# The gate column multiplied with the keys instead of the values, and the gate row loaded and transposed later

## Chip, cores, metric

One core of one Trainium2 chip. The metric is the device time of one execution in microseconds (us).

## The reference, cut to what matters

```python
# x: [1, 2048, 640]; 32 heads of 20
g = sigmoid((x * gate_w).sum(-1, keepdims=True))      # one number per token
a = A(x, wqkv, w_phi, wo)     # linear attention: q, k, v projections, softmax features of q and k
b = B(x, w_gate, w_up, w_down)                        # SwiGLU feed-forward, 640 -> 1728 -> 640
return g * a + (1 - g) * b
```

The gate needs one dot product of length 640 per token. The kernel gets it nearly free: gate_w is appended as a 641st column to a weight matrix that multiplies x anyway. The question is which matrix carries the column, and when the column is made.

## The kernel before

Tokens come in 16 tiles of 128. For each tile a projection is ten matmuls: five chunks c of the contraction, two halves of 320 columns each. The value weights wvg carry the gate column, so the second half of a value tile has 321 columns. The premultiplied key and query weights lie together in wqk. Of a matmul's two operands the token chunk xT is loaded first (LDWEIGHTS, engine PEld in the views) and the strip of wvg or wqk is read by the matmul itself: it is the moving operand. The result goes to PSUM (ps in the views), a memory apart from SBUF, where the operands lie. The row pitch is the distance from one chunk's row to the next: 640 elements of 2 bytes, or 642 where there is room for the gate column.

```python
LOADS = "x0 w0 x1 g w1 x2 w2 x3 w3 w4 f0 h ..."        # x: tokens, w: wv rows, g: gate row
ORDER = "... H12 X0 G X1 U0.0 U1.0 U0.1 X2 U1.1 U2.0 ... X3 ... U2.4 V3 Y F0.1 M1 ..."
# H warm-up, X transpose of a token tile, G of the gate row, U a chunk of a value tile,
# V a value tile, F feed-forward, M premultiply of the keys, K key tile, Q query tile
...
wqk = sb("wqk", [P, 2, 5, D], BF16)
wvg = sb("wvg", [P, 5, D + 2], BF16)
...
XQ = ["sp", "act", "act", "act"]                       # queues of x0..x3
WQ = ["act", "sp", "sp", "sp", "act"]                  # queues of w0..w4
def load_gate():
    dma("sp", gwr[0:5, :], ...)                        # 5 rows of 128
def gcol():
    transposes([(o, gwr[0:5, :])], 5)
    copy("dve", wvg[:, :, D:D + 1], o.unsqueeze(2))
def v_pairs(t, pr):
    return [(bank(2 * pr + hb, 0, 320 + hb), xT[:, t, c, :], wvg[:, c, 320 * hb:640 + hb - 320 * (1 - hb)],
             c == 0, c == 4, False) for c in range(5) for hb in range(2)]
def v_out(t, pr):
    copy("act", o, i)                                  # values out of PSUM
    copy("act", svec[:, t:t + 1], bank(2 * pr + 1, 320, 321))   # the gate's column
def tok_proj(t, which, split=False):                   # which: 1 keys, 0 queries
    pairs = [(bank(2 * pr + hb, 0, 320), xT[:, t, c, :], wqk[:, which, c, 320 * hb:320 * hb + 320],
              c == 0, c == 4, False) for c in range(5) for hb in range(2)]
```

The softmax here doesn't subtract the row's maximum and nothing guards it: scores larger than these inputs give would overflow.

## Time and profile before

| | before |
|---|---|
| time, median of 3 executions | 288.73 us (288.58 to 288.88) |
| span of the profiled execution | 287.0 us |
| TensorE busy | 284.1 us |
| granted TensorE clock | 1.0 |
| third token tile x2 landed, its transposes began | 5.91 us, 5.95 us |
| first feed-forward matmul to the end of the last matmul | 273.88 us |

The lines of the profile are in the prediction below. The chain of work that ended last has, as columns, start, length (both us) and what ran; after the short transpose of the z row it ends with one unbroken piece of TensorE work, 13 of the 16 query tiles and most of the feed-forward.

```profile
77.45 0.06 PE ps L308
77.51 207.57 PE ps L296 x1275
```

Because the piece is unbroken, its length (207.57 us) is a sum of matmul distances.

### The profile page before, as it was taken

To read this page: it belongs to the slowest core of one execution; us is meant where nothing else is said; L and a number is where in the kernel's file an instruction comes from. 1 tells how busy PE (TensorE), PEld (TensorE's weight loads), DVE (VectorE), ACT (ScalarE), POOL (GpSimd) and SP (SyncE) were. 2 spreads that over 40 slices of the span, in tenths; PEclk is the share of its full clock that TensorE was granted. 3 is DMA by queue.
4 is the path that set the end of the run, shared out by engine and by line. 5 is a ranking of instruction groups with operands and counts; after the bars stand their busy time and mean duration, and the time that the engine had idled before them with its cause. 6 is when DMAs were issued, how large, how long until landed. Compare 5 with 4: busy or idle time off the path is not lost.

```text
span 287.0 us, 4972 instructions
## 1 busy us (share of the span) xinstructions
PE 284.1 (99%) x1979; PEld 174.5 (61%) x1979; DVE 163.3 (57%) x243; ACT 152.4 (53%) x256; POOL 159.8 (56%) x125
## 2 busy tenths in 40 slices
PE   8999999999999999999999999999999999999997
PEld 6667777575644545557775556675554446666776
DVE  2337748576569978689991465970317899100000
ACT  0767778576775465683535753225676552234112
POOL 8286999879446789836543438350754558501000
PEclk9999999999999999999999999999999999999999
DMA  7977697000010598202383002061020006210101
GB/s 234 192 113 127 113 279 279 3 1 2 0 50 0 123 290 162 50 2 50 66 157 69 6 1 50 2 149 43 2 50 0 3 1 123 53 46 0 49 23 48
DMA packets 48944, 21.62 MB, mean 75 GB/s; under 512 B 39384, under 2 KB 48792, under 8 KB 48920
## 3 DMA queue, kind: packets, MB, share of 16 engines
q1 hardware_dynamic: 47400, 20.43, 31.5%
q10 hardware_dynamic: 1520, 0.87, 1.0%
q8 instruction: 16, 0.26, 0.4%
q14 instruction: 8, 0.07, 0.1%
HBM read 9.29 MB, written 2.62 MB: 42 GB/s over the span
## 4 chain that ended last, share of the span: by engine, by line
PE 99%; DVE 0%; issue 0%
PE ps L296 97%; PE ps L478 1%; PE ps L308 0%; DVE xT L320 0%; DVE osb L737 0%; DVE wvg L320 0%
## 5 line engine op out<-in xcount | busy, mean ns | idle before, releaser
L324 POOL TENSOR_TENSOR hT<-hT,us 128x512 bf16<-128x512 bf16 (+1 forms) x56 | 65.0, 1174 | 65.1 <-DVE hT L328 47.5
L328 DVE SCALAR_TENSOR_TENSOR hT<-hT,ps 128x512 bf16<-128x512 bf16 (+1 forms) x56 | 37.4, 683 | 66.8 <-ACT hT L314 53.0
L296 PE MATMUL ps<-xT,wg 128*128 128x512 bf16 x260 | 64.6, 379 | 0.0
L296 PE MATMUL ps<-xT,wu 128*128 128x512 bf16 x260 | 64.6, 379 | 0.0
L296 PE MATMUL ps<-wd,hT 128*128 128x320 bf16 (+2 forms) x462 | 63.9, 295 | 0.0
L324 POOL TENSOR_TENSOR ph<-eq,qc 128x1320 bf16<-128x1320 bf16 x16 | 42.4, 2647 | 25.6 <-DVE qc L638 20.8
L296 PEld LDWEIGHTS ps<-wd,hT 128*128 128x128 bf16 x462 | 44.5, 98 | 17.5 <-issue 0.2
L296 PE MATMUL ps<-wqk,xT 128*128 128x320 bf16 x320 | 47.7, 299 | 0.0
L314 ACT ACTIVATE hT<-ps 128x512 bf16<-128x512 f32 (+2 forms) x64 | 36.4, 569 | 16.8 <-PE ps L296 16.5
L296 PEld LDWEIGHTS ps<-xT,wu 128*128 128x128 bf16 x260 | 25.5, 98 | 30.6
L314 ACT ACTIVATE us<-ps 128x512 bf16<-128x512 f32 (+1 forms) x56 | 33.5, 598 | 18.5 <-PE ps L296 17.3
L314 ACT ACTIVATE osb<-ps,omg 128x640 bf16<-128x640 f32 (+2 forms) x17 | 12.9, 758 | 55.4 <-PE ps L296 55.4
L296 PEld LDWEIGHTS ps<-xT,wg 128*128 128x128 bf16 x260 | 25.1, 98 | 27.8 <-ACT osb L314 0.8
L324 POOL TENSOR_TENSOR ekr<-ekr,krec 128x1280 bf16<-128x1280 bf16 x16 | 37.4, 2358 | 5.8 <-DVE krec L338 5.8
L296 PEld LDWEIGHTS ps<-wqk,xT 128*128 128x128 bf16 x320 | 30.5, 98 | 13.1 <-issue 0.4
L314 ACT ACTIVATE eq<-ps 128x640 bf16<-128x640 f32 x32 | 22.4, 704 | 20.9 <-POOL ph L324 10.8
L335 DVE TENSOR_REDUCE ksum<-ekr 128x64 f32<-128x1280 bf16 x16 | 23.5, 1471 | 11.7 <-ACT ekr L314 11.7
L314 ACT ACTIVATE ekr<-ps 128x640 bf16<-128x640 f32 x32 | 22.3, 704 | 8.7 <-PE ps L296 8.2
L335 DVE TENSOR_REDUCE qz<-eq 128x64 f32<-128x1280 bf16 x16 | 23.6, 1478 | 2.6 <-ACT eq L314 2.6
L296 PE MATMUL ps<-wog,oT 128*128 128x320 bf16 (+2 forms) x165 | 24.7, 294 | 0.0
L296 PE MATMUL ps<-wvg,xT 128*128 128x320 bf16 (+1 forms) x160 | 24.1, 299 | 0.1
L335 DVE TENSOR_REDUCE qw<-ez 128x64 f32<-128x1280 bf16 x16 | 23.6, 1477 | 0.0
(73 smaller groups left out, 188.6 us busy)
## 6 DMA issues: line engine op xcount, KB each, us to landing
out_dram<-osb SPq DMA_DIRECT2D x15, 160.0 KB, 2.0
wd<-in_B_w_down_dram SPq DMA_DIRECT2D x1, 2080.0 KB, 9.2
wg<-in_B_w_gate_dram SPq DMA_DIRECT2D x1, 1040.0 KB, 10.0
wu<-in_B_w_up_dram SPq DMA_DIRECT2D x1, 1040.0 KB, 12.2
wg<-in_B_w_gate_dram SPq DMA_DIRECT2D x1, 800.0 KB, 6.1
wu<-in_B_w_up_dram SPq DMA_DIRECT2D x1, 800.0 KB, 7.7
wog<-in_A_wo_dram SPq DMA_DIRECT2D x2, 375.0 KB, 7.1
xs<-in_A_x_dram ACTq DMA_DIRECT2D x3, 160.0 KB, 4.2
```

The source lines that it names most:

```text
L296: last = pe.matmul(o, lhsT=l, rhs=r, start=st, stop=sp_, skip_group_check=sk)
L314: return run("act", lambda: act.activation(o, i, func, scale=scale), rd, [o])
L324: return run(e, lambda: eo.tensor_tensor(o, a, b, op), [a, b], [o])
L328: return run("dve", lambda: dve.scalar_tensor_tensor(out=o, in0=a, scalar=s, in1=b, op0=op0, op1=op1), rd, [o])
L335: return run("dve", lambda: dve.tensor_reduce(o, i, AX.X, ALU.add), [i], [o])
L478: last = pe.matmul(bank(2 * pr, 0, P), lhsT=c, rhs=c, start=True, stop=True)
```

## The change

The intent: take the gate row, its transpose and its copy out of the start, where the first value matmul waits for them. The value tiles start first, so the column has to go where it is needed later, to the keys.

```diff
-x0 w0 x1 g w1 x2 w2 x3 w3 w4 f0 h k0 ...
+x0 w0 x1 w1 x2 w2 x3 w3 w4 g f0 h k0 ...
-H0 ... H12 X0 G X1 U0.0 U1.0 U0.1 X2 ...
+H0 ... H12 X0 X1 U0.0 U1.0 U0.1 X2 ...
-X3 U2.2 U0.3 U1.3 U2.3 U0.4 U1.4 U2.4 V3 Y F0.1 ...
+X3 U2.2 U0.3 U1.3 U2.3 U0.4 U1.4 U2.4 V3 G Y F0.1 ...
-    wqk = sb("wqk", [P, 2, 5, D], BF16)
-    wvg = sb("wvg", [P, 5, D + 2], BF16)
+    wqk = sb("wqk", [P, 2, 5, D + 2], BF16)
+    wvg = sb("wvg", [P, 5, D], BF16)
 def load_gate():
-        dma("sp", gwr[0:5, :], ...)
+        dma("act", gwr[0:5, :], ...)
 def gcol():
-        copy("dve", wvg[:, :, D:D + 1], o.unsqueeze(2))
+        copy("dve", wqk[:, 1, :, D:D + 1], o.unsqueeze(2))
 # v_pairs: plain halves of 320; v_out: no svec copy
 # tok_proj: second half 320 + which columns
 def ktile(t):
         head_exps(pr, e)
+        copy("act", svec[:, t:t + 1], bank(2 * pr + 1, 320, 321))
 # premult writes wqk[:, which, m, 0:D]
 def kv_end():
+        for _ in range(2):
+            sp.wait_ge(tr.sem["pe"], 1)
```

## The prediction

> **What bounds the kernel now.** I read the page first: the busy line and the chain that ended last.
>
> ```profile
> span 287.0 us, 4972 instructions
> ...
> PE 284.1 (99%) x1979; PEld 174.5 (61%) x1979; DVE 163.3 (57%) x243; ACT 152.4 (53%) x256; POOL 159.8 (56%) x125
> ...
> PEclk9999999999999999999999999999999999999999
> ...
> PE 99%; DVE 0%; issue 0%
> ```
>
> TensorE is at work for 284.1 of 287.0 us, at full clock, and the chain is TensorE's own program. The other engines have 40% idle each. A busy TensorE may still hide waits, so next the chain in order of time:
>
> ```profile
> 3.77 0.72 PE ps L308 x5
> 4.50 0.02 issue
> 4.52 0.42 DVE xT L320
> 4.94 0.10 DVE wvg L320
> 5.04 0.05 issue
> 5.09 1.00 PE ps L296 x6
> 6.08 0.32 PE ps L308 x5
> 6.40 1.37 PE ps L296 x10
> 7.78 0.28 PE ps L308 x5
> 8.05 69.40 PE ps L296 x640
> ```
>
> After 8 us the chain never leaves TensorE, except for 0.4 us at the very end. I also took the start-to-start distance of every neighbouring pair of matmuls: beyond the usual distance of their kind, only 0.94 us is lost after 8 us, about 0.1 us at a time around the small attention-output matmuls, which this change does not touch. So time can be won only in two places: in waits before 6 us, or in the rate at which matmuls follow each other. The timeline of TensorE gives that rate. A duration (second column) includes the drain of the pipeline, so the distance of the starts (first column) is what counts:
>
> ```profile
> 26.99 1.54 PE L296 MATMUL ps<-wvg,xT 128*128 128x320 bf16 x10
> 28.37 1.52 PE L296 MATMUL ps<-wqk,xT 128*128 128x320 bf16 x10
> 29.72 0.51 PE L296 MATMUL ps<-v1r,ekr 128*128 128x63 bf16 x11
> ```
>
> A value tile (on wvg) takes 28.37 - 26.99 = 1.38 us, a key tile (on wqk) 29.72 - 28.37 = 1.35, though both are ten matmuls and differ by one column in five of them.
>
> **What the Trainium skill says.** "TensorE: Matmul & The Clock Gate", section "Back-to-back issue gap", gives N/2.4 + 2.5 ns for the isolated gap between warm matmuls: 135.8 ns for 320 columns, 136.2 for 321. The trace agrees: key and query matmuls start 135 or 136 ns apart. So the extra column explains 5 x 0.42 = 2 ns of a value tile, not its whole excess. "SBUF — State Buffer", section "Specifications (TRN2)", says that SBUF has 16-byte cachelines and each cross to a new line pays a penalty. The row pitch of wvg is 642 elements = 1284 bytes = 80 x 16 + 4, so chunks c = 0 to 4 of a value tile begin at 0, 4, 8, 12 and 0 bytes into a line (the tensor itself begins on a multiple of 32). Averaged over the twelve value tiles after 15 us, the two halves of these chunks take 135.5/136.6, 139.8/139.3, 138.3/139.3, 138.5/139.3 and 135.0/136.0 ns. Exactly the three chunks that begin off a line pay some 3 ns per matmul: a match in this trace, though the page gives no figure for a matmul. "DMA: Bandwidth & Descriptors", section "Issuing engines are not separate DMA queues", says that transfers of all issuing engines share the 16 DMA engines, and only issue time is saved by spreading them. Here an issue takes 0.4 us on its queue, and that is what moves.
>
> **The change part by part.**
>
> 1. The column moves from the value to the key weights, and with it the odd pitch. The ten matmuls of a value tile sum to 1377.3 ns, of a key or query tile (pitch 640) to 1358.2.
>  - Values, now pitch 640 and 320 columns: 16 x (1358.2 - 1377.3) = **-0.30 us**.
>  - Keys are the second half of wqk and begin 5 x 1284 = 6420 bytes in, 4 past a line. Their chunks begin at 4, 8, 12, 0, 4: four of five are off. With the measured figures of the same offsets: 2 x (139.8 + 139.3) + 138.3 + 139.3 + 138.5 + 139.3 + 135.2 + 136.3 = 1385 ns. 16 x (1385 - 1358.2) = **+0.43 us**.
>  - Queries have no extra column but share the pitch: offsets 0, 4, 8, 12, 0, six matmuls some 2.8 ns slower, 16.5 ns a tile, 16 tiles: **+0.26 us**.
>  All of this lies on the path, as TensorE is the path. Sum: +0.39 us. No matmul is added or removed.
>
> 2. The gate transpose leaves the start:
>
> ```profile
> 4.41 0.18 PE L308 MATMUL ps<-ident,gwr 5*128 5x5 bf16 x1
> 4.53 0.45 PE L308 MATMUL ps<-ident,xs 128*128 128x128 bf16 x5
> 5.09 1.00 PE L296 MATMUL ps<-wvg,xT 128*128 128x320 bf16 x6
> 5.95 0.45 PE L308 MATMUL ps<-ident,xs 128*128 128x128 bf16 x5
> ```
>
> It stands at 4.41 where TensorE had paused since 4.27, and the next transposes start 0.11 us later. Its copy into wvg (0.17 us on VectorE, to 5.03) releases the first value matmul:
>
> ```profile
> 5.08 0.66 PEld L296 LDWEIGHTS ps<-wvg,xT 128*128 128x128 bf16 x6 [0.28 <-DVE wvg L320]
> 5.95 0.28 PEld L308 LDWEIGHTS ps<-ident,xs 128*128 128x128 bf16 x5 [0.20 <-DMA xs<-in_A_x_dram]
> ```
>
> Without both, that matmul starts some 0.25 us sooner. But the third tile's transposes then wait for x2 until 5.95, as now (landed 5.91), so the gain survives only if x2 lands earlier. Its issue does not move. What moves is w1, issued at 1.66 behind the gate row and then at 1.25. Landings now: x1 4.26, w1 5.47, x2 5.91, w2 6.34, x3 7.05, w3 7.29, w4 7.79. From 5.47 on a 160 KB block lands every 0.46 us, but the 1.2 us between x1 and w1 hold only one: there is slack, and w1 sooner should pull all that follows by up to 0.4 us (x1 itself may lose 0.1 to 0.2, as w1 now shares with it). I take **-0.25 us**, anything from 0 to -0.4 being possible.
>
> 3. The transpose between the fourth value tile and the first feed-forward tile: five-column work that cannot cover the next weight load. Its distance to the next start was 0.11 us; the similar transpose of the z row has 0.057. I take **+0.08 us**. Its copy (0.17 us) falls where VectorE idles before wbd (2.8 us idle), and keys start 7 us later.
>
> 4. On ScalarE the column read moves from behind each value copy to behind each key's two exponentials:
>
> ```profile
> L314 ACT ACTIVATE svec<-ps 128x1 f32<-128x1 f32 x16 | 2.8, 174 | 0.0
> ```
>
> Same sixteen; each delays the next ScalarE operation by only 0.05 us (10.07 to 10.12), but holds its PSUM pair some 0.12 us longer. Where TensorE in this stage reuses a pair read by ScalarE, it starts at least 0.37 us after that read ended, except two matmuls of the first key tile that wait for premultiplied weights. 0 us.
>
> 5. The two added waits of the sync engine are already satisfied and stand where it has nothing urgent: 0 us.
>
> Sum: +0.39 - 0.25 + 0.08 = +0.22 us; 288.73 + 0.22 = 288.95, so **288.9 us**.
>
> **The rivals.** (a) *The start gain is whole and the pitch costs nothing*: if the slow value matmuls were due to the column, the cost would only move to the keys, and -0.25 to -0.4 us plus 0.08 would leave about 288.5. Against it: 320-column halves of the off-line chunks are slow too, 138 to 140 ns. (b) *The start gives nothing*: x2 lands as late as now, or x1 later because w1 competes. Then 288.73 + 0.47 = 289.2. For it: x2's issue is unchanged, DMA engines are busy from 4 us on. (c) *A new wait in the key stage*: the longer hold of the key's PSUM pair makes TensorE wait. If each of 16 key tiles cost 0.1 us: +1.6 us, about 290.5. Against it: slack of 0.37 us, and value pairs come free 0.15 us sooner. (d) *The premultiply of the keys becomes the limit of the start*: its block weights are finished at 12.95 and it starts at 13.13, so a start more than 0.2 us sooner would wait for them, unless their source, issued after w3's landing, is sooner too, as I expect. It would cap the gain near 0.2.
>
> **Range and chances.** The terms are a few tenths; the pitch term is measured to within 0.1 us, the start is the loose one (0 to -0.4), and three runs spread by 0.3 us. (b) and (a) mark 289.2 and 288.5; with a little room for (c) and for effects of shifted instruction fetches, 288.3 to 289.5. Two per cent is 5.8 us: nothing in the trace can move that much. Faster 0.005, within 0.985, slower 0.01.
>
> **What would show it.** Step 1: value tiles start-to-start 1.36 us, keys 1.385, queries 1.375; matmuls of chunk 3 of the keys the only fast ones. Step 2: first value matmul near 4.8, x2 landing near 5.6, its transposes near 5.7. Step 3: a 5-column transpose near 11 us with at most 0.11 us behind it. Step 4: no wait of TensorE for ScalarE between 20 and 75 us. It would be wrong if key and query tiles still took 1.358 us, or if the trace showed TensorE gaps in the key stage.

## The result

In four executions the changed kernel took 288.87 us in the median (288.70 to 289.71), before 288.81 (288.58 to 289.17, four executions). A ratio here is the mean time of one kernel's runs over the mean of the other's runs of the same rounds, so it is not quite the ratio of the medians quoted: 1.0007, 95% interval 0.9984 to 1.0029. Executions over 1.5% slower than the fastest of the same kernel are left out of the means. Two later repeats of the unchanged pair, on two chips and told below, gave 1.0032 (1.0008 to 1.0056) and 1.0034 (1.0021 to 1.0047). So the three comparisons put the cost between nothing and a third of a per cent, and no interval reaches beyond 0.6 per cent: well within the 2 per cent.

The page of the changed kernel's profiled execution (289.01 us) says at once where to look:

```profile
span 287.8 us, 4972 instructions
...
PE 284.6 (99%) x1979; PEld 174.6 (61%) x1979; DVE 163.6 (57%) x243; ACT 152.2 (53%) x256; POOL 159.8 (56%) x125
...
PE 97%; DMA 2%; ACTq 0%; DVE 0%; issue 0%
```

TensorE is still the bound, but it has 0.5 us more work, and a DMA has entered the chain that was TensorE's alone. The same chain in order of time, from its first transfer on:

```profile
...
1.73 4.53 DMA xs<-in_A_x_dram
...
6.30 0.45 PE ps L308 x5
...
8.39 3.26 PE ps L296 x24
11.65 0.11 PE ps L308
11.76 66.36 PE ps L296 x616
...
78.17 207.71 PE ps L296 x1275
```

The first long piece of the chain is now the transfer of x2, which lands at 6.26 us instead of 5.91, and the third tile's transposes begin at 6.30 instead of 5.95. The gate transpose appears at 11.65 as a piece of its own. The last piece is 207.71 us instead of 207.57: 0.14 us more, and the 13 query tiles in it, which gained no column, take 11 ns more each.

The same stretch of TensorE's timeline as in the prediction, one value tile, one key tile, and what follows:

```profile
27.54 1.52 PE L296 MATMUL ps<-wvg,xT 128*128 128x320 bf16 x10
28.89 1.54 PE L296 MATMUL ps<-wqk,xT 128*128 128x320 bf16 x10
30.28 0.50 PE L296 MATMUL ps<-v1r,ekr 128*128 128x63 bf16 x11
```

From start to start the value tile is now 1.35 us and the key tile 1.39; before it was 1.38 and 1.35. And the weight loads of TensorE, with the idle time ahead of each and what ended it in brackets:

```profile
4.70 0.45 PEld L308 LDWEIGHTS ps<-ident,xs 128*128 128x128 bf16 x5 [0.57 <-DMA xs<-in_A_x_dram]
...
6.30 0.28 PEld L308 LDWEIGHTS ps<-ident,xs 128*128 128x128 bf16 x5 [0.41 <-DMA xs<-in_A_x_dram]
...
11.58 0.09 PEld L308 LDWEIGHTS ps<-ident,gwr 5*128 5x128 bf16 x1 [0.26 <-issue]
11.69 0.76 PEld L296 LDWEIGHTS ps<-xT,wg 128*128 128x128 bf16 x5
```

The wait for the gate's copy is gone, as intended, but the second tile's transposes now wait 0.57 us for x1, and the third tile's 0.41 for x2 (0.20 before). At 11.58 there is a pause of 0.26 us ahead of the gate's small weight load.

From the third tile's transposes to the end of the last matmul the profiled executions took 279.12 us before and 279.56 after, +0.44. The start of those transposes adds the other +0.35. These are the two sums to explain.

### The profile page after: what moved, and what is told of

Same layout as the page of the kernel before. It is cut to its first block, busy times and chain, and to the rows that moved or that the text cites. A ratio compares the mean times of both kernels' runs of the same rounds, so it can differ in the third digit from the quotient of the medians.

```text
span 287.8 us, 4972 instructions
## 1 busy us (share of the span) xinstructions
PE 284.6 (99%) x1979; PEld 174.6 (61%) x1979; DVE 163.6 (57%) x243; ACT 152.2 (53%) x256; POOL 159.8 (56%) x125
## 4 chain that ended last, share of the span: by engine, by line
PE 97%; DMA 2%; ACTq 0%; DVE 0%; issue 0%
PE ps L296 97%; DMA xs<-in_A_x_dram 2%; PE ps L308 0%; ACTq L350 0%; DVE osb L738 0%
## 5 line engine op out<-in xcount | busy, mean ns | idle before, releaser
L296 PE MATMUL ps<-wvg,xT 128*128 128x320 bf16 x160 | 23.9, 299 | 0.0
```

The source lines that it names most:

```text
L296: last = pe.matmul(o, lhsT=l, rhs=r, start=st, stop=sp_, skip_group_check=sk)
```

## The experiments

Three questions were open: whether the distance between matmuls is set by the row pitch or by the extra column; why the start did not gain; and what the late transpose costs. **Theory**: a moving operand that begins off a 16-byte line costs some 3 ns per matmul; w1, issued 0.4 us sooner, takes transfer time from x1 and x2; and the small transpose costs TensorE time wherever it stands. **Rivals**: the column's width is what costs; landings only scatter from one execution to the next; the pause at 11.58 belongs to its place.

Twelve runs were made, three of them of unchanged kernels, in four groups. Runs of a group shared a chip and the runs of before, five rounds each; where nothing else is said, an edit is to the kernel named in its diff. All results were correct. This table puts together the readings; landings and starts are in us from the start of the span of each run's profiled execution. F is the start of the first feed-forward matmul, "F to end" the time from there to the end of the last matmul; "w1" tells when w1 was issued.

| run | w1 | x1 landed | x2 landed | F | F to end | median | before beside it | ratio (95%) |
|---|---|---|---|---|---|---|---|---|
| before | 1.66 | 4.26 | 5.91 | 11.19 | 273.88 | 288.73 | | |
| after | 1.24 | 4.66 | 6.26 | 11.69 | 274.17 | 288.87 | 288.81 | 1.0007 (0.9984 to 1.0029) |
| e1_line | 1.24 | 4.86 | 7.08 | 12.52 | 273.72 | 289.01 | 288.48 | 1.0017 (1.0005 to 1.0029) |
| e2_pitch | 1.66 | 4.17 | 6.03 | 11.41 | 274.28 | 289.23 | 288.48 | 1.0022 (1.0010 to 1.0034) |
| e3_wd | 1.66 | 4.37 | 6.24 | 11.63 | 274.48 | 289.32 | 288.48 | 1.0028 (1.0011 to 1.0044) |
| e4_aa | 1.66 | 4.06 | 5.71 | 10.99 | 273.89 | 288.76 | 288.48 | 1.0006 (0.9992 to 1.0019) |
| e5_loadback | 1.66 | 4.30 | 5.80 | 11.40 | 274.17 | 289.00 | 288.52 | 1.0015 (1.0000 to 1.0030) |
| e6_again | 1.24 | 4.89 | 6.77 | 12.21 | 274.16 | 289.42 | 288.52 | 1.0032 (1.0008 to 1.0056) |
| e7_wvgline | 1.66 | 4.29 | 6.28 | 12.25 | 273.69 | 288.36 | 288.52 | 0.9995 (0.9981 to 1.0010) |
| e8_both | 1.66 | 4.42 | 5.66 | 11.41 | 273.72 | 288.45 | 288.52 | 0.9993 (0.9979 to 1.0007) |
| e9_x2first | 1.72 | 4.62 | 4.41 | 12.12 | 273.72 | 289.00 | 288.56 | 1.0019 (1.0007 to 1.0031) |
| e10_w1wait | 1.67 | 4.35 | 5.85 | 11.75 | 274.17 | 289.07 | 288.56 | 1.0015 (1.0003 to 1.0027) |
| e11_third | 1.27 | 4.81 | 5.70 | 11.34 | 274.17 | 289.34 | 288.56 | 1.0034 (1.0021 to 1.0047) |
| e12_gap | 1.67 | 4.45 | 5.59 | 11.23 | 273.72 | 288.34 | 288.56 | 0.9989 (0.9970 to 1.0009) |

Look first at "F to end". It repeats to 0.01 us for kernels with the same matmuls (274.16 or 274.17 in all five profiles of the changed kernel's body), while F itself moves between 11.34 and 12.21 for one and the same kernel. In these profiles the scatter is in the start, and nearly all that the pitch does (all but the first four value tiles) is in the rigid rest. So the two are judged apart. Only the profiled execution of each run shows its landings; of the others the time alone is known.

### e1_line: the pitch of wqk on a line

```diff
-    wqk = sb("wqk", [P, 2, 5, D + 2], BF16)   # in the changed kernel
+    wqk = sb("wqk", [P, 2, 5, D + 8], BF16)
```

> The changed kernel with the row pitch of wqk at 648 elements (1296 bytes, 81 lines of 16 bytes) instead of 642; the gate column still goes with the keys. Theory (start off a 16-byte line costs some 3 ns a matmul): every key and query tile is back at 1357 to 1361 ns from start to start (after: 1381 and 1371), so the stretch from the first feed-forward matmul to the last is 0.55 us shorter than in the changed kernel. Rival (the 321st column or the wider strip itself costs): key tiles stay near 1381 ns and nothing is won there. Second rival (a 32-byte line): odd chunks stay slow. Total against before: within 0.1 per cent either way, since the start may be late.

Key tiles took 1361.8 ns, query tiles 1358.1 (after: 1381.2 and 1370.7; the query figures here are of the 14 tiles without another pause in them). In the chain the two long pieces became:

```profile
12.58 66.04 PE ps L296 x616
...
78.68 207.57 PE ps L296 x1275
```

66.36 became 66.04, and 207.71 became 207.57, exactly the figure of before. The rigid part fell by 0.45 us (274.17 to 273.72), less than the 0.55 expected. The column itself costs 4 ns a tile (1361.8 against 1357.5), the pitch 19. Chunks that begin 16 bytes past a multiple of 32 are as fast as the others, so the step that counts here is 16 bytes, not 32. The whole time, however, did not fall: x2 landed at 7.08 in the profile.

### e2_pitch: the pitch alone, in the kernel before

```diff
-    wqk = sb("wqk", [P, 2, 5, D], BF16)       # in the kernel before
+    wqk = sb("wqk", [P, 2, 5, D + 2], BF16)
 # premult writes wqk[:, which, m, 0:D]
```

> The kernel before with one edit: wqk has the row pitch 642, no column is moved and the gate stays where it was. Theory: key tiles 1379 to 1381 ns and query tiles 1371 ns instead of 1357.5 and 1358.7, value tiles stay at 1377; the sum is +0.55 us, all of it after 18 us, nothing at the start. Rival (column width is the cause): key and query tiles unchanged, 0 us.

No matmul changed its width, and still key tiles went to 1374.4 ns and query tiles to 1370.7, with values at 1376.2. The chain's pieces, against 69.40 and 207.57 before:

```profile
8.28 69.67 PE ps L296 x640
...
78.01 207.70 PE ps L296 x1275
```

F to end rose by 0.40 us. The rival, width, is out; the size expected (0.55) was too large. The single distances say why. In a key tile here, chunks begin 4, 8, 12, 0 and 4 bytes into a line, and the ten matmuls took 135.0, 139.2, 138.5, 138.4, 138.3, 139.4, 135.0, 135.1, 135.4 and 140.0 ns. Eight are off a line, but the first of each run of them goes at the full rate. Only where a 321-column matmul stands ahead is that first one slow too, as in the value tiles of before (139.8) and in the fifth chunk of the changed kernel's keys (139.3). The prediction had charged all of them.

### e3_wd: the same pitch elsewhere, as a magnifier

```diff
-    wd = sb("wd", [P, 14, D], BF16)           # in the kernel before
+    wd = sb("wd", [P, 14, D + 2], BF16)       # and wd[:, k, 0:D] wherever it is used
```

> A magnifier: the kernel before with the row pitch of wd, the moving operand of the down projection, at 642 instead of 640 elements; nothing else. Ten of its 14 chunks then begin off a 16-byte line, 20 of 38 matmuls of an output tile. Theory: about 3 ns each, 60 ns a tile, +0.9 us over 16 tiles (range 0.7 to 1.2), seen as 138 to 140 ns from start to start. Rival (the effect belongs to these weights or to the projection stage): 135.9 ns as before, 0 us.

The first long piece stays, the second grows:

```profile
8.50 69.39 PE ps L296 x640
...
77.94 208.19 PE ps L296 x1275
```

+0.62 us (from 207.57), all in the matmuls with wd: the sum of their distances went from 60.95 to 61.56 us. The effect belongs to the moving operand's address, not to one tensor. It is under the expected 0.7 to 1.2, by the same rule: 20 of the 38 matmuls of a tile are off a line, the first of each of four runs free, so 16 pay: 38 ns a tile, 2.4 ns each. (The first of the last run, a matmul of 104 rows, takes 139 to 140 ns with either pitch.)

### e4_aa: the kernel before, once more

> The kernel before once more, unchanged: how far its own time and its own landings scatter. Theory (late x2 in the changed kernel comes from the earlier issue of w1): x2 lands near 5.9 us again, and the third tile's transposes begin near 5.95. Rival (landings scatter from run to run): x2 lands anywhere between 5.5 and 6.5 us. Time ratio to before 1.000 within 0.001.

Ratio 1.0006, F to end 273.89 against 273.88. x2 landed at 5.71 here and at 5.91 in the first profile, and the executions of the kernel before ranged from 288.01 to 289.80 us. A difference of 0.1 per cent in one comparison of times is therefore no evidence.

### e5_loadback: the gate row loaded ahead of w1 again

```diff
-x0 w0 x1 w1 x2 w2 x3 w3 w4 g f0 h ...        # in the changed kernel
+x0 w0 x1 g w1 x2 w2 x3 w3 w4 f0 h ...
-    dma("act", gwr[0:5, :], ...)
+    dma("sp", gwr[0:5, :], ...)
```

> The changed kernel with the gate row loaded again by the sync engine ahead of w1; transpose and column stay where the change put them. Theory (w1 issued 0.4 us sooner shares with x1 and x2 and makes x2 late): x1 lands near 4.2, w1 at 4.8 to 5.9, x2 at 5.7 to 6.25 us as in the kernels with the old start, the third tile's transposes begin between 5.75 and 6.4, and from there to the last matmul's end it takes 279.6 us as in the changed kernel; time about 0.3 us under the changed kernel. Rival (landings only scatter): x2 lands as late as 6.3 to 7.1.

x1 at 4.30, x2 at 5.80, F at 11.40, F to end 274.17. The mean was 0.53 us under the unchanged changed kernel beside it (288.96 against 289.49), more than expected, but under two standard errors (0.39 us), and the one execution of 291.17 us makes much of it. The expected 279.6 us from the third tile's transposes to the end were 279.70.

### e6_again and e11_third: the changed kernel, unchanged, twice

> The changed kernel once more, unchanged, for the scatter of its start. Theory: x2 lands at 6.25 us or later again (6.26 and 7.08 in the two profiles with the new start so far, 5.71 to 6.24 in the four with the old); transposes of the third tile at 6.3 or later; from there to the end 279.56 us as before. Rival (scatter): x2 lands as early as 5.7 to 6.0.

> The changed kernel a third time, on the chip of the two runs beside it. Theory: x1 lands at 4.6 to 4.9 and x2 at 6.25 to 7.1; from the first feed-forward matmul to the end 274.17 us; 0.1 to 0.4 per cent over before. Rival (scatter): x1 under 4.4 and x2 under 6.0.

e6_again agreed: x1 4.89, x2 6.77, and the widest scatter of all (288.62 to 291.17 us). e11_third agreed on x1 (4.81), on F to end and on the time, but not on x2. In its weight loads one sees the third tile going without a wait:

```profile
4.85 0.28 PEld L308 LDWEIGHTS ps<-ident,xs 128*128 128x128 bf16 x5 [0.72 <-DMA xs<-in_A_x_dram]
5.83 0.40 PEld L308 LDWEIGHTS ps<-ident,xs 128*128 128x128 bf16 x5
```

x2 had landed at 5.70, as early as with the old start; this execution (288.65 us) was also the fastest of its six, the others taking 289.09 to 290.08. So the theory in the form "x2 always lands late" falls. What remains is the time: both means stood 0.9 us over before.

### e10_w1wait: w1 late, without the gate row ahead of it

```diff
 def load_wv(c):                               # in the changed kernel
+    if c == 1:
+        sp.wait_ge(tr.sem["pe"], 3)
```

> The changed kernel with one wait of the sync engine ahead of w1, for the third warm-up item of TensorE (some 1.8 us), so that w1 is issued about as late as before, but with no gate row ahead of it. Theory (the issue time of w1 is what matters, not the gate row): w1 is issued at 1.6 to 1.9, x1 lands near 4.1 to 4.4 and x2 at 5.6 to 6.3; the third tile's transposes begin before 6.4. From the first feed-forward matmul to the end 274.17 us. Time 0.3 us or more under the unchanged repeat beside it. Rival (the small gate row itself, or scatter): x1 near 4.7, x2 at 6.3 to 7.1 as in the changed kernel.

w1 was issued at 1.67, and x1 landed at 4.35. The second tile's transposes followed the first tile's without a wait of their own, so the ten stand as one entry:

```profile
3.82 1.02 PEld L308 LDWEIGHTS ps<-ident,xs 128*128 128x128 bf16 x10 [0.32 <-DMA xs<-in_A_x_dram]
```

For x1 the issue time of w1 decides, not the gate row. The whole came out 0.41 us under e11_third beside it (means 288.94 and 289.35, standard error 0.24), although in the profiled execution x3 was late (7.95) and F only at 11.75.

### e7_wvgline and e8_both: versions that could be faster

```diff
 # e7_wvgline, in the kernel before
-    wvg = sb("wvg", [P, 5, D + 2], BF16)
+    wvg = sb("wvg", [P, 5, D + 8], BF16)
```

> The kernel before with one edit: the row pitch of wvg is 648 instead of 642 elements, so every chunk begins on a 16-byte line; nothing else. Theory: value tiles take 1361 to 1362 ns (321 columns on a line) instead of 1377; from the third tile's transposes to the end 278.85 us instead of 279.12, so the time is 0.25 us under before if the start is equal. Rival: value tiles stay at 1377, 0 us.

```diff
 # e8_both, in the changed kernel: e1_line and e5_loadback together
-    wqk = sb("wqk", [P, 2, 5, D + 2], BF16)
+    wqk = sb("wqk", [P, 2, 5, D + 8], BF16)
-x0 w0 x1 w1 x2 w2 x3 w3 w4 g f0 h ...
+x0 w0 x1 g w1 x2 w2 x3 w3 w4 f0 h ...
-    dma("act", gwr[0:5, :], ...)
+    dma("sp", gwr[0:5, :], ...)
```

> The changed kernel with both costs undone: the row pitch of wqk at 648 and the gate row loaded by the sync engine ahead of w1; the column still goes with the keys and the transpose stands behind the fourth value tile. Theory: from the third tile's transposes to the end 279.1 us (as in the run with pitch 648 alone), x2 lands at 5.7 to 6.25, so the time equals before within 0.2 us: the late transpose costs what the aligned values win. Rival (the start is only scatter): a late start, x2 over 6.3, time 0.3 us or more over before.

e7_wvgline: value tiles 1361.9 ns, F to end 273.69, 0.19 us under before (twelve value tiles lie behind F). The expected 278.85 us from the third tile's transposes were 279.30, because in that execution w2 landed at 7.82 and x3 at 8.23. e8_both: 279.10 us from there, as expected, and 0.2 us under before in the mean. In the whole time neither differs from before beyond the scatter.

### e9_x2first: x2 issued in w1's place

```diff
 # in e1_line
-x0 w0 x1 w1 x2 w2 ...
+x0 w0 x2 x1 w1 w2 ...
-XQ = ["sp", "act", "act", "act"]
-WQ = ["act", "sp", "sp", "sp", "act"]
+XQ = ["sp", "act", "sp", "act"]
+WQ = ["act", "act", "sp", "sp", "act"]
-X0 X1 U0.0 U1.0 U0.1 X2 U1.1 U2.0 U0.2 ...
+X0 X1 U0.0 U1.0 X2 U2.0 U0.1 U1.1 U0.2 ...
```

> A version that should beat both at the start: the changed kernel with wqk's row pitch at 648, and x2 issued second on the sync engine in w1's place (w1 third on the other queue in x2's place), the third tile's transposes and its first value chunk moved ahead of the chunk that needs w1. Theory (a block lands by its place in the issue order): x2 lands at 4.4 to 4.9 us as w1 did there, w1 at 5.5 to 6.5; the first feed-forward matmul starts at 11.0 to 11.5 us (12.52 in the run with pitch 648 alone) and from it to the last matmul's end it takes 273.72 us as there; time 0.2 to 0.8 us under the changed kernel, equal to before or up to 0.3 us better. Rival (landing is scatter, whatever the order): x2 lands at 6.2 to 7.1.

x2 landed at 4.41, exactly where w1 had landed in the changed kernel, and w1 at 6.65, a little late: the landing follows the place in the order. x1 was no sooner (4.62), with x2 now issued beside it at 1.25. But nothing was won over before. F came at 12.12 instead of the expected 11.0 to 11.5, because now TensorE waited for w1, and then the fourth tile for x3:

```profile
6.70 1.20 PEld L296 LDWEIGHTS ps<-wvg,xT 128*128 128x128 bf16 x10 [0.52 <-DMA wvg<-in_A_wqkv_dram]
8.37 0.28 PEld L308 LDWEIGHTS ps<-ident,xs 128*128 128x128 bf16 x5 [0.47 <-DMA xs<-in_A_x_dram]
```

x3 landed at 8.32 there. Pulling x2 forward pushed w1 back. That it pushed x3 back too is not shown: x3 came as late in e7_wvgline (8.23), where the order was the old one.

### e12_gap: the gate transpose in a pause

```diff
 # in e8_both
-U0.0 U1.0 U0.1 X2 ... V3 G Y F0.1
+U0.0 U1.0 U0.1 G X2 ... V3 Y F0.1
```

> The run with both costs undone (wqk pitch 648, gate row ahead of w1), and the gate transpose moved from behind the fourth value tile into the pause in which TensorE waits for x2 anyway. Theory (the late transpose costs 0.2 us on the path, the same work in a pause costs nothing): from the third tile's transposes to the first feed-forward matmul 5.18 us instead of 5.38, from there to the end 273.72; value and key tiles 1357.8 and 1361.8 ns; time 0.2 us under that run and some 0.3 us (0.1 per cent) under before, if the landings are equal. Rival (the pause behind the fourth value tile belongs to the next tile, not to the transpose): 5.38 us stays.

From the third tile's transposes to F it was 5.19 us, as expected, but the reading was badly chosen. The weight loads:

```profile
5.93 0.09 PEld L308 LDWEIGHTS ps<-ident,gwr 5*128 5x128 bf16 x1 [0.26 <-issue]
6.04 0.28 PEld L308 LDWEIGHTS ps<-ident,xs 128*128 128x128 bf16 x5
```

x2 had landed at 5.59, and the last value matmul ahead began at 5.706, so without the gate transpose the third tile's would have begun at 5.84 (136 ns later). They began at 6.04. The 0.20 us were moved ahead of the point from which I counted, not hidden; here no pause was left to hide them in. The rival, that the pause belongs to the place behind the fourth value tile, is out all the same: the pause of 0.26 us went with the transpose. The time, 0.9989 of before (0.9970 to 1.0009), is the lowest ratio but not distinguishable from 1.

## Why the prediction was right, and where it was not

The predicted 288.9 us met the measured 288.87, and the range held. But three terms of the sum were off: the pitch was put too high, the start and the late transpose too low. The predicted difference was +0.22 us; the first medians differ by +0.06, the means of the later repeats by +0.85 and +0.91, the profiled pair by +0.79. So the agreement is partly luck, and the steps are to be read apart.

**Step 1, the pitch: the mechanism was right and is shown** (e1_line takes it away, e2_pitch puts it alone into the kernel before, e3_wd puts it elsewhere). The sizes were off. The predicted terms were -0.30 for values, +0.43 for keys and +0.26 us for queries. Measured per tile, and times 16: values 1377.3 to 1356.6 ns, -0.33; keys 1357.5 to 1381.2, +0.38; queries 1358.1 to 1370.7, +0.20 (an expectation above has 1358.7 for the queries before; the 14 tiles without another pause give 1358.1). The sum is **+0.25 instead of +0.39**. Most of the excess was the charge for the first off-line matmul of a run, which in these traces pays nothing unless a 321-column one precedes it. The column itself costs 4 ns a tile, where the prediction had 2.

**Step 2, the start: wrong.** The prediction took -0.25 us, for x2 landing up to 0.4 us sooner once w1 no longer queued behind the gate row. In the profiled pair w1 did land sooner (4.41 instead of 5.47), but x2 later (6.26), and the first value matmul, forecast near 4.8, began at 5.22 (5.09 before). The step that failed is the slack between x1 and w1: the prediction had allowed x1 to lose 0.1 to 0.2. In the profiles x1 landed at 4.66 to 4.89 us with the early w1 of the changed kernel (four profiles) and at 4.06 to 4.45 where no other 160 KB block was issued at 1.25 beside it (nine profiles, the wait of e10_w1wait among them); in e9_x2first, where x2 took that place, it landed at 4.62. That is shown, and it is some 0.5 us. The Trainium skill, "DMA: Bandwidth & Descriptors", section "Queues, rings and completion order", says that each DMA engine takes turns between the queues that have work for it, packet by packet; x1 and w1, issued at the same 1.25 us on two queues, then share, which agrees with both landing within 0.3 us of each other (4.41 and 4.66). The traces show the sharing: from 3.0 to 3.5 us the packets of ScalarE's queue, which carries x1, took 84% of the 16 engines' time before, and 89% in e5_loadback and e10_w1wait, but 40, 41 and 53% in the three profiles of the changed kernel, while all queues together moved 0.18 to 0.20 MB in each. For x2 the picture is only a tendency: 6.26, 6.77, 7.08 and 5.70 with the early w1, 5.59 to 6.28 with the late one. In time, the changed kernel stood 0.53 and 0.41 us over its two twins with w1 issued late (e5_loadback, e10_w1wait), with standard deviations of 0.3 to 0.9 us over the five or six executions of each; neither difference is two standard errors. e1_line and e8_both, which differ in the same way, stood 0.53 us over and 0.20 under the before beside each, but on two chips. All three comparisons point one way: the early issue probably costs about half a microsecond on average, in place of the predicted gain, but no pair on one chip shows it. Nor is it settled that x2 is the block through which it costs. TensorE can wait for others: 0.45 us for x3 in e10_w1wait, 0.57 for w2 in e7_wvgline, both with the late w1.

**Step 3, the late transpose: under-sized.** Predicted +0.08 us, measured **+0.20**. The distance behind the transpose was 0.106 us, as forecast (at most 0.11); what was left out is the pause ahead of it. The last value matmul ahead of it began at 11.356 us in the changed kernel, the gate's weight load only at 11.584, 228 ns later, where weight loads elsewhere in that stretch begin 1 or 2 ns after the matmul ahead starts. The first feed-forward matmul began 0.338 us after that value matmul instead of 0.136. The transpose of the z row, from which I drew the estimate, has 120 rows and shows no such pause. The skill's "TensorEngine Tiling (Array Packing)", section "Tiling Modes", says that changing the tiling mode drains TensorE. A load of 5 rows among loads of 128 may be such a change; the trace fits, but no run tried another number of rows. The kernel before already had the same pause ahead of another load of a different shape, 120 rows by 64 columns, in the attention output:

```profile
153.63 0.90 PEld L296 LDWEIGHTS ps<-phiT,kvsb 120*64 120x64 bf16 x12 [0.26 <-issue]
```

It too began 227 ns after the matmul ahead. The time lost around these matmuls, some 0.1 us at each end of the group, which the prediction had seen and set aside as untouched by the change, was a better guide than the z row. In the kernel before there was a like pause ahead of the transpose (0.20 us at 4.41), but the wait for x2 until 5.95 swallowed it.

**Step 4, ScalarE's column read at the keys, and step 5, the added waits: 0, as predicted.** F to end of e1_line, which has both, is 273.72 us. From before's 273.88, twelve value tiles lose 19.5 ns each (to 1357.8), 0.23 us, and sixteen key tiles gain 4.3, 0.07 us: 273.72. Nothing is left over for a wait.

Together: +0.25 and +0.20 meet the +0.44 us from the third tile's transposes on to 0.01 us. The start of those transposes, +0.35 in the profiled pair, makes the rest of the +0.79.

Of the rivals in the prediction, (b), a start that gives nothing, 289.2 us, came nearest: the later repeats had medians of 289.42 and 289.34. But their own distance from before, +0.85 and +0.91 us by the means, is more than its +0.47. Rival (a), a pitch that costs nothing, is refuted; (c), a wait in the key stage, did not occur; (d), the premultiply as a limit, was never tested, since the start never came early enough.

## What to carry to other kernels

An extra column in a matmul's moving operand is nearly free (4 ns in 1358 here), but not if it spoils the row pitch: pad the pitch to a multiple of 16 bytes, or the neighbours pay (here the queries, which had no column at all). Work taken out of a start is worth only as much as the next wait lets through, and issuing one block sooner can delay the block that TensorE waits for first (here x1, by some 0.5 us). When the whole time scatters by more than the effect, find the stretch in which the bounding engine runs without a break, and compare its length.

## What the Trainium skill lacked or had wrong

- "SBUF — State Buffer", section "Specifications (TRN2)", has the 16-byte lines but no figure for a matmul. Here a 320-column bf16 moving operand that begins 4, 8 or 12 bytes into a line takes 138 to 140 ns instead of 135 to 136, except for the first of a run of them; one that begins 16 bytes off a 32-byte boundary pays nothing.
- "TensorE: Matmul & The Clock Gate", section "Back-to-back issue gap", gives N/2.4 + 2.5 ns as the isolated gap and about 131 ns per matmul as sustained at N = 512. In these runs 512-column matmuls in long streams with weight loads between start 215 or 216 ns apart at clock 1.0, which is the isolated figure (215.8), not the sustained one.
- "TensorEngine Tiling (Array Packing)", section "Tiling Modes", gives no figure for the drain. One 5-row transpose in a stream of 128-row work cost 0.20 us here, its weight load starting 228 ns after the matmul ahead began, and the loads of 120 rows by 64 columns started 227 ns after theirs; whether it is that drain, no run shows.
- No page tells how far landings scatter at the start of a kernel. The same 160 KB block of the same kernel, issued at 1.72 to 1.74 us, landed at 5.70, 6.26 and 6.77 us in three executions.
